# A pre-LN transformer block on one core: x loaded in eight parts, the prologue's statistics and evacuations dealt out anew, a PSUM bank held back

## The chip, the core and the metric

The kernel runs on one core of a Trainium2 chip. The metric is device time in microseconds (us) of one execution, median of several runs. A core has TensorE (PE in the profile; PEld is its weight load), VectorE (DVE), ScalarE (ACT), GpSimd (POOL) and SyncE (SP), which here issues every DMA. The engines run side by side, each takes its own instructions in order, and semaphores tie them together.

## The reference

Sequence 2048, width 640, 32 heads of 20, all in bfloat16:

```python
h  = x + softmax(q k^T / sqrt(20)) v @ wo      # q, k, v = layernorm(x) @ wqkv
h2 = h + (gelu(g) * u) @ w_down                # g, u = layernorm(h) @ w_gate, w_up (width 1728)
```

## The kernel before, in words

**A planner writes the order.** The function declares operations (engine, planned duration, priority, what is read and written, which PSUM banks are taken) and `Sched.schedule` (line 102) plays them out with planned times, taking on each engine the ready operation of lowest priority number; `emit` writes each engine's instructions in that order with the semaphore waits needed. The order is fixed when the kernel is built: on the chip an engine whose next instruction is not ready waits, even if a later one is. Most constants at the file's head are arguments of this planner. A tuple has one value per slot (below).

**Prologue.** x arrives in parts (`load_x`, line 608, in the order `XORD`), then wqk, wv and wo. x is 16 tiles of 128 rows. Tiles are normalised by `GROUPS`: first the statistics of a group, then one reciprocal root for all of it (ScalarE does the root), then each tile is normalised by VectorE (`ln_apply`, "apply" below), transposed by TensorE (line 675) into PSUM and copied out by ScalarE (line 681) or, for the tiles in `XN_DVE`, by VectorE (line 684). Statistics come from VectorE (`bn_stats` twice and `bn_aggr`) at the lowest priority, `P_BG`; for the group `AG` they come from ScalarE (`act_stats`, line 718: a Copy and a Square with an accumulated sum per tile). Warm matmuls (`WN` of them, line 620) fill TensorE before real work. Then the K projection of head block 0 (four chunks of 512 rows, line 758; chunk c needs tiles 4c to 4c+3), copied out by ScalarE (line 795); the largest |K| per row comes from VectorE (line 792), before the copy from PSUM for chunks in `KPS`, after it from SBUF for the others; with `KCUT` chunk 3 is done in two pieces. The maximum over all chunks gives a bound on the scores (`kd`, `sel0`, `q_bound0`), after which the first scores can be computed.

**Slots.** Attention runs in 32 slots: query chunks of 512, 256 (five) and 128 (two) rows by groups of four heads. A slot has 64 score tiles of 128x512, all from line 1081. They are grouped into units of three and two PSUM banks in turn (0 to 2, then 3 and 4); ScalarE computes the exponential of a unit in one instruction. `D_SLOT` blocks of four tiles per slot go to VectorE instead, which builds the exponential from integer arithmetic (line 992 from PSUM, then four terms, each needing its own product with V; `SUMS` says how many pairs VectorE adds first). A VectorE tile is put into a unit's third bank (a "ring", `D_RING` of a slot's twelve) or into a free bank of 5 and 7; those banks also serve all background work: K, Q and V projections, the output projection and the feed-forward of the query chunk before (`post`). `RESV` is a time: where the next unit has a VectorE tile in a bank of its own and is due sooner than that, TensorE takes no other work that would leave banks 5 and 7 without a free one. At 0 the rule is off.

**Tail.** After the last slot, output projection and feed-forward of the last 128 rows.

Of the kernel before, what the change touches and what calls it, by code (L numbers as in the profile page):

```python
# [18 lines left out]
DRAIN = {"pe": 0.165, "act": 0.118, "dve": 0.085, "pool": 0.05, "sp": 0.0}  # L19
WARM_WIN, WARM_MIN = 3.4, 0.5  # L20
PAD_WIN, PAD_MIN = 3.4, 0.42
QK_LEAD = (0.68, 0.72,) + (0.65,) * 4 + (0.72,) * 7 + (0.6,) * 4 + (0.72,) * 6 + (0.68, 0.68, 0.55, 0.55, 0.68, 0.65, 0.65, 0.68, 0.68,)
ACT_GAP = .012
PE_AGE = (2.5,) + (3.0,) * 5 + (5.0,) * 8 + (3.0,) * 3 + (5.0, 5.0, 2.0, 2.0,) + (5.0,) * 4 + (1.5, 1.5, 3.5, 3.0,) + (1.5,) * 3
SD_AGE = (0.6, 0.6, 0.3,) + (0.6,) * 6 + (0.8,) + (0.6,) * 5 + (1.0, 0.3, 0.6, 0.8, 0.6, 1.0, 0.5, 1.0, 1.0, 0.5,) + (0.6,) * 3 + (0.8,) * 4
SD_ROW = (0,) * 5 + (0.6,) * 4 + (1.5, 0.6, 0.6, 1.5,) + (0.6,) * 16 + (1.0, 0.6, 0,)
STOP = None


# [336 lines left out]
NTERM = len(TERMS)  # L366
PV_QUADS = 2
PR, PR2 = 13, 6
D_SLOT = (1,) + (3,) * 26 + (2, 3, 3, 0, 0,)
SUMS = (0,) + (1,) * 4 + (2, 2, 0, 0, 1, 0,) + (1,) * 3 + (0, 1, 1, 2, 3, 1, 0, 1, 1, 0, 2, 2, 1, 0, 1, 0, 3, 0,)  # L370
HOP = 3.2
D_LAT = 0.3
RECIP_MAGIC = float(0x7EF311C3)
COL = 256
WN, WB, WW, WC = 76, (5, 4), 256, 32
KCUT = (384,)
KPS = (2, 3)
P_KM = 1.52
P_VA = 9
RESV = 0.0  # L380
QK_LAT = 0.165
VN = 4
D_RING = (9,) * 4 + (6, 6,) + (9,) * 6 + (6,) * 16 + (12,) + (6,) * 3
D_FIRST = 0
D_SPAN = (16,) + (18,) * 13 + (17,) + (18,) * 4 + (19,) * 4 + (18,) * 7 + (17, 17,)
# [40 lines left out]
LATE = (0, 1, 2, 3, 4)  # L426

# [1 line left out]
def bass_sequential_preLN__mha_block__glu_gated_geglu__prompt_kernel(  # L429
# [10 lines left out]
    x_hbm = A_x[0]  # L440
    out_hbm = out[0]
    with ExitStack() as es:
# [123 lines left out]
        def cst(fn, key, n=128):  # L566
# [149 lines left out]


        def act_stats(t0, n):
            for t in sorted(range(t0, t0 + n), key=lambda t: (XORD.index(t // 4), t)):
                for f, k in ((ACT.Copy, 0), (ACT.Square, 1)):  # L720
                    op("act", I("activation", junk, x_sb[:, t, :], f, accum_out=asum[:, k, t - t0:t - t0 + 1]), 0.86, 1.4,
                       reads=[f"x{t // 4}"], writes=["junk", ("as", t)])
            m = mv[:, t0:t0 + n, 0]
            rk = [("as", t) for t in range(t0, t0 + n)]
            d = lambda fn, r, w: op("dve", fn, 0.17, P_RS, reads=r, writes=w)
            d(I("tensor_scalar", m, asum[:, 0, 0:n], 1.0 / D, None, ALU.mult), rk, ["am"])
            d(I("tensor_tensor", asum[:, 0, 0:n], m, m, ALU.mult), ["am"], rk)
# [194 lines left out]
        for c, (q0, nq) in enumerate(CHUNKS):  # L922
            n = 512 // nq
# [22 lines left out]
        while rem:  # L946
# [3 lines left out]
            k = in_slot.setdefault(s_, [0, 0])  # L950
# [4 lines left out]
            n = len(bs)  # L955
# [567 lines left out]
```

## Time and profile before

| | us |
|---|---|
| median of 3 runs (lowest, highest) | 866.83 (866.38, 867.52) |
| the profiled execution's own time | 867.75 |
| its span, first to last instruction | 866.0 |
| ScalarE busy | 838.4 (97%) |
| TensorE busy | 838.5 (97%) |
| VectorE busy | 750.4 (87%) |

Two engines are busy for 97% of the span. A busy TensorE is not one at its peak (its matmuls overlap and some are fill). Three stretches are to be kept apart: the prologue, up to the first exponential; the slots; the tail.

### The profile page before, as it was taken

The page shows a single profiled execution, that of the slowest core. Times are in us where ns is not written, and L with a number is a line of the kernel's source. Part 1 is how long each engine was busy: PE and PEld are TensorE (multiplying, and loading weights), DVE is VectorE, ACT ScalarE, POOL GpSimd, SP SyncE. Part 2 cuts the span into 40 slices and gives each one's busy share as a digit, 9 for nine tenths or more (in the row PEclk, how much of TensorE's full clock was granted, in tenths as well). Part 3 has the DMA queues.
Part 4 walks back from the last instruction along what each step waited for, and adds up shares of the span by engine and source line. Part 5 has one row for each costly group of instructions (what it writes and reads, how often), then busy time and mean ns, then how long its engine had stood idle before and what let it go on. Part 6 is the DMA issues. An engine that isn't in the chain of part 4 may idle for free.

```text
span 866.0 us, 35545 instructions
## 1 busy us (share of the span) xinstructions
PE 838.5 (97%) x16215; PEld 420.4 (49%) x16215; DVE 750.4 (87%) x1372; ACT 838.4 (97%) x806; POOL 89.6 (10%) x268
## 2 busy tenths in 40 slices
PE   7999999999999899999999999999999999999998
PEld 5532332322343344445455555555554556666667
DVE  8769999999999799797899989999999897988344
ACT  7999999999999999999999999999999999999992
POOL 5001111110001110101002000011102110010000
PEclk9999999999999999999999999999999999999999
DMA  7212021223202642001110102010101101030000
GB/s 274 81 47 61 29 76 47 59 61 92 58 16 60 160 147 80 16 18 36 53 42 16 36 8 61 5 35 17 49 19 24 58 12 27 20 47 11 2 18 17
DMA packets 50173, 43.19 MB, mean 50 GB/s; under 512 B 21316, under 2 KB 44640, under 8 KB 50024
## 3 DMA queue, kind: packets, MB, share of 16 engines
q1 hardware_dynamic: 50024, 40.93, 16.8%
q8 instruction: 127, 2.08, 1.0%
q14 instruction: 22, 0.18, 0.1%
HBM read 27.95 MB, written 10.26 MB: 44 GB/s over the span
## 4 chain that ended last, share of the span: by engine, by line
ACT 51%; PE 39%; DVE 8%; issue 1%
ACT pts L450 35%; ACT rege L450 15%; PE ps L1081 11%; PE ps L450 10%; PE ps L753 9%; PE ps L758 3%; DVE qt_all L450 2%; DVE rege L450 2%; PE ps L907 1%; PE ps L1336 1%; DVE rege L992 1%; DVE qt_all L992 1%; PE ps L1405 1%; ACT qt_all L450 1%; PE ps L675 1%
## 5 line engine op out<-in xcount | busy, mean ns | idle before, releaser
L450 ACT ACTIVATE pts<-ps 128x1024 bf16<-128x1024 f32 (+1 forms) x496 | 558.5, 1240 | 2.8 <-PE ps L1081 2.2
L1081 PE MATMUL ps<-qt_all,kt_all 32*128 32x256 bf16 (+2 forms) x4096 | 304.0, 273 | 11.5 <-ACT pts L450 5.6
L450 ACT ACTIVATE rege<-ps 128x1024 bf16<-128x1024 f32 (+1 forms) x222 | 248.3, 1199 | 0.7 <-PE ps L1081 0.3
L1081 PEld LDWEIGHTS ps<-qt_all,kt_all 32*128 32x128 bf16 x4096 | 103.2, 92 | 202.8 <-ACT pts L450 90.6
L992 DVE TENSOR_SCALAR rege<-ps 128x512 int16<-128x512 f32 x220 | 148.5, 684 | 20.0 <-PE ps L1081 18.6
L450 PE MATMUL ps<-rege,v_all 128*21 128x256 bf16 (+2 forms) x2197 | 139.3, 286 | 0.5 <-DVE rege L450 0.5
L450 PE MATMUL ps<-pts,v_all 128*21 128x256 bf16 (+2 forms) x2403 | 124.8, 273 | 1.0 <-DVE osb L450 0.8
L753 PE MATMUL ps<-rege,regw 128*32 128x256 bf16 (+1 forms) x2600 | 120.5, 296 | 1.6 <-DVE rege L992 0.5
L992 DVE TENSOR_SCALAR qt_all<-ps 128x512 int16<-128x512 f32 x128 | 86.7, 683 | 11.0 <-PE ps L1081 10.2
L450 DVE TENSOR_SCALAR rege<-rege 128x2048 int16<-128x2048 int16 x141 | 94.5, 687 | 1.5 <-PE ps L450 0.8
L753 PEld LDWEIGHTS ps<-rege,regw 128*32 128x32 bf16 x2600 | 60.4, 96 | 34.6 <-issue 20.1
L450 PEld LDWEIGHTS ps<-rege,v_all 128*21 128x21 bf16 x2197 | 54.4, 91 | 41.6 <-issue 26.1
L450 PEld LDWEIGHTS ps<-pts,v_all 128*21 128x21 bf16 x2403 | 56.6, 91 | 26.0 <-issue 19.2
L450 DVE TENSOR_SCALAR qt_all<-qt_all 128x2048 int16<-128x2048 int16 (+4 forms) x113 | 65.4, 589 | 3.0 <-ACT qt_all L450 1.0
L753 PE MATMUL ps<-regw,rege 128*32 128x320 bf16 x1296 | 67.4, 301 | 0.3 <-DVE rege L992 0.3
L758 PE MATMUL ps<-regw 128*128 128x512 bf16 (+2 forms) x215 | 59.6, 368 | 0.4
L450 PE MATMUL ps<-qt_all,v_all 128*21 128x256 bf16 (+1 forms) x1264 | 56.5, 264 | 0.8 <-DVE qt_all L450 0.8
L450 DVE TENSOR_SCALAR qt_all<-rege 128x2048 int16<-128x2048 int16 x80 | 53.8, 684 | 1.6 <-PE ps L450 1.2
L450 POOL TENSOR_SCALAR rn<-rc 128x16 int32<-128x16 int32 x22 | 7.0, 317 | 461.7 <-DMA rc<-sums 461.6
L1390 DVE TENSOR_TENSOR rege<-rege,ps 128x512 bf16<-128x512 bf16 (+2 forms) x53 | 35.0, 661 | 13.0 <-PE ps L753 6.6
L1336 PE MATMUL ps<-rege,regw 128*128 128x128 bf16 (+1 forms) x420 | 40.9, 238 | 0.0
L753 PEld LDWEIGHTS ps<-regw,rege 128*32 128x32 bf16 x1296 | 30.0, 96 | 18.3 <-issue 10.8
(139 smaller groups left out, 805.7 us busy)
## 6 DMA issues: line engine op xcount, KB each, us to landing
bsum<-rsums SPq DMA_DIRECT2D x88, 64.0 KB, 2.1
rege<-in_A_x_dram SPq DMA_DIRECT2D x5, 640.0 KB, 5.8
q_rows<-regw SPq DMA_DIRECT2D x20, 128.0 KB, 1.8
out_dram<-rege SPq DMA_DIRECT2D x15, 160.0 KB, 1.8
regw<-in_B_w_gate_dram SPq DMA_DIRECT2D x5, 432.0 KB, 3.3
regw<-in_B_w_up_dram SPq DMA_DIRECT2D x5, 432.0 KB, 3.5
kt_all<-k_rows SPq DMA_DIRECT2D x12, 160.0 KB
qt_all<-q_rows SPq DMA_DIRECT2D x12, 160.0 KB
```

The costliest lines, as they stand in the source:

```text
L450: return lambda eng: getattr(eng, method)(*args, **kwargs)
L675: op("pe", lambda eng, a=a: eng.transpose(bank16(bk, D)[:, 128 * a:128 * a + 128], src[:, a * 128:(a + 1) * 128], ident[:]), 0.055, prio, ...
L753: return [lambda eng, j=j: eng.matmul(out()[32 * j:32 * j + 32], l[:, 32 * j:32 * j + 32], r, start=start, stop=stop, tile_position=(0, 32 ...
L758: fn = col4(lambda: bank(bk, n), l, r, k == 0, k == len(steps) - 1) if col else lambda eng, l=l, r=r, k=k: eng.matmul(bank(bk, n), l, r, s ...
L907: w_readers.append(op("pe", lambda eng, i=i, kt=kt, a=a: eng.matmul(bank(bk)[:, i * w:i * w + w], xnT[:, a, kt * 128:(kt + 1) * 128], wv[: ...
L992: d_ops.append(op("dve", lambda eng: eng.tensor_scalar(v[:, 512 * h:512 * h + 512], bank(b), EXP_MUL, -32000.0, ALU.mult, ALU.max), c_dve( ...
L1081: return lambda eng: eng.matmul(out()[:, kk * nq:(kk + 1) * nq], kt_all[32 * j:32 * j + 32, g, kt * 128:(kt + 1) * 128], qt_all[32 * j:32 ...
L1336: lambda eng, a=a, f=f, fi=fi: eng.matmul(bank(bk)[:, fi * nq:(fi + 1) * nq], w[:, a, F0[f]:F0[f] + 128], hnT[:, a, 128 * tb:128 * tb + nq ...
L1390: hdone.append(op("dve", lambda eng, bu=bu, fv=fv, w=w: eng.tensor_tensor(fv, fv, bank(bu, w), ALU.mult), c_dve(w), p, reads=[ku] + hkeys( ...
L1405: f == NF - 1) if cl else lambda eng, f=f, o=o, bk=bk, w0=w0, w1=w1: eng.matmul(
```

## The change

All of it is in constants and in the loading of x: no function is new and the planner's code is the same.

- **x in eight parts** of 256 rows in the order 0, 6, 1, 7, 2, 3, 5, 4 (before: four parts of 512 rows in the order 0, 3, 1, 2); a tile's statistics wait for its own part.
- **Statistics.** ScalarE has tiles 12 to 15 (before 11 to 15), VectorE 0 to 11 in groups of four and eight (before 0 to 10, in groups of four and seven).
- **Transposed tiles** 4, 6, 7, 10, 13 and 14 are copied out by VectorE (before 7, 10, 13 and 15).
- **K projection** of block 0: chunk 3 in one piece, and only its maximum is taken from PSUM. The projection of block 1 may start after chunk 1's copy (before: after chunk 3's), its first chunk copied by ScalarE. 60 warm matmuls (before 76).
- **Slots.** Slot 0 gives two blocks to VectorE (before one); more rings in slots 0 and 6 to 10; slot 14 has the pair sum that slot 9 had. `RESV` is 0.4 us. The first query chunk's normalised h is transposed by TensorE (before by DMA). Per-slot lead times and waiting times of the planner (`QK_LEAD`, `PE_AGE`, `SD_AGE`, `SD_ROW`) and several priorities have other values.

```diff
-QK_LEAD = (0.68, 0.72,) + (0.65,) * 4 + (0.72,) * 7 + (0.6,) * 4 + (0.72,) * 6 + (0.68, 0.68, 0.55, 0.55, 0.68, 0.65, 0.65, 0.68, 0.68,)
+QK_LEAD = (0.68, 0.75,) + (0.65,) * 4 + (0.72,) * 6 + (0.68,) + (0.72,) * 3 + (0.6,) * 9 + (0.8,) * 3 + (0.72,) + (0.8,) * 3
...
-D_SLOT = (1,) + (3,) * 26 + (2, 3, 3, 0, 0,)
+D_SLOT = (2,) + (3,) * 26 + (2, 3, 3, 0, 0,)
...
-WN, WB, WW, WC = 76, (5, 4), 256, 32
-KCUT = (384,)
-KPS = (2, 3)
+WN, WB, WW, WC = 60, (5, 4), 256, 32
+KCUT = ()
+KPS = (3,)
...
-RESV = 0.0
+RESV = 0.4
...
-VN = 4
-D_RING = (9,) * 4 + (6, 6,) + (9,) * 6 + (6,) * 16 + (12,) + (6,) * 3
+VN = 1
+D_RING = (8,) + (9,) * 3 + (6, 6,) + (12,) * 4 + (9, 9,) + (6,) * 16 + (12, 6, 6, 4,)
...
-P_EV = 1.8
+P_EV = 1.5
...
-XN_DVE = (7, 10, 13, 15)
+XN_DVE = (4, 6, 7, 10, 13, 14)
...
-XP_PE = (6,)
+XP_PE = (0, 6)
-P_KP = 1.6
-K1_AFTER = 3
-Q1_HOLD = 1
-V_HOLD = 3
+P_KP = 1.5
+K1_AFTER = 1
+Q1_HOLD = 0
+V_HOLD = 6
...
-K1_ACT = ()
+K1_ACT = (0,)
...
-GROUPS = ((0, 4), (4, 7), (11, 5))
-AG = (11, 5)
-P_RS = 1.45
-XORD = (0, 3, 1, 2)
+GROUPS = ((0, 4), (4, 8), (12, 4))
+AG = (12, 4)
+P_RS = 1.0
+XORD = (0, 6, 1, 7, 2, 3, 5, 4)
...
-P_ADD = 1.8
+P_ADD = 0.6
...
-P_OUT = 2.5
+P_OUT = 1.1
...
-            load(x_sb[:, 4 * i:4 * i + 4, :], x_hbm[512 * i:512 * (i + 1), :].rearrange("(t p) d -> p t d", p=128),
-                 f"x{i}", 5.1 + 1.8 * k)
+            load(x_sb[:, 2 * i:2 * i + 2, :], x_hbm[256 * i:256 * (i + 1), :].rearrange("(t p) d -> p t d", p=128),
+                 f"x{i}", 4.2 + 0.9 * k)
```

More of the change, by code (lines that the diff above doesn't have):

```diff
@@ L21 @@
 PAD_WIN, PAD_MIN = 3.4, 0.42
-QK_LEAD = (0.68, 0.72,) + (0.65,) * 4 + (0.72,) * 7 + (0.6,) * 4 + (0.72,) * 6 + (0.68, 0.68, 0.55, 0.55, 0.68, 0.65, 0.65, 0.68, 0.68,)
+QK_LEAD = (0.68, 0.75,) + (0.65,) * 4 + (0.72,) * 6 + (0.68,) + (0.72,) * 3 + (0.6,) * 9 + (0.8,) * 3 + (0.72,) + (0.8,) * 3
 ACT_GAP = .012
-PE_AGE = (2.5,) + (3.0,) * 5 + (5.0,) * 8 + (3.0,) * 3 + (5.0, 5.0, 2.0, 2.0,) + (5.0,) * 4 + (1.5, 1.5, 3.5, 3.0,) + (1.5,) * 3
-SD_AGE = (0.6, 0.6, 0.3,) + (0.6,) * 6 + (0.8,) + (0.6,) * 5 + (1.0, 0.3, 0.6, 0.8, 0.6, 1.0, 0.5, 1.0, 1.0, 0.5,) + (0.6,) * 3 + (0.8,) * 4
-SD_ROW = (0,) * 5 + (0.6,) * 4 + (1.5, 0.6, 0.6, 1.5,) + (0.6,) * 16 + (1.0, 0.6, 0,)
+PE_AGE = (2.5, 3.0, 5.0, 5.0, 2.5, 2.5,) + (3.0,) * 7 + (3.5,) * 4 + (5.0, 5.0, 3.5, 3.5, 5.0,) + (1.5,) * 3 + (5.0,) + (3.0,) * 4 + (1.5, 1.5,)
+SD_AGE = (0.6, 0.6, 0.3,) + (0.6,) * 6 + (0.8,) + (0.6,) * 6 + (0.3, 0.6, 0.8, 0.6, 1.0, 0.5, 1.0, 1.0, 0.5, 0.6, 0.6, 0.8, 0.8,) + (0.6,) * 3
+SD_ROW = (0,) * 5 + (1.0, 0, 0.6, 0.6, 1.5, 0.6, 0.6, 1.5, 0.6, 0,) + (0.6,) * 5 + (0.3, 0.6, 0, 0, 0.6, 0.6, 0.3, 0.6, 0.6,) + (1.0,) * 3
 STOP = None
@@ L368 @@
 PR, PR2 = 13, 6
-D_SLOT = (1,) + (3,) * 26 + (2, 3, 3, 0, 0,)
-SUMS = (0,) + (1,) * 4 + (2, 2, 0, 0, 1, 0,) + (1,) * 3 + (0, 1, 1, 2, 3, 1, 0, 1, 1, 0, 2, 2, 1, 0, 1, 0, 3, 0,)
+D_SLOT = (2,) + (3,) * 26 + (2, 3, 3, 0, 0,)
+SUMS = (0,) + (1,) * 4 + (2, 2,) + (0,) * 4 + (1,) * 6 + (2, 3, 1, 0, 1, 1, 0, 2, 2, 1, 0, 1, 0, 1, 0,)
 HOP = 3.2
@@ L374 @@
 COL = 256
-WN, WB, WW, WC = 76, (5, 4), 256, 32
-KCUT = (384,)
-KPS = (2, 3)
+WN, WB, WW, WC = 60, (5, 4), 256, 32
+KCUT = ()
+KPS = (3,)
 P_KM = 1.52
 P_VA = 9
-RESV = 0.0
+RESV = 0.4
 QK_LAT = 0.165
-VN = 4
-D_RING = (9,) * 4 + (6, 6,) + (9,) * 6 + (6,) * 16 + (12,) + (6,) * 3
+VN = 1
+D_RING = (8,) + (9,) * 3 + (6, 6,) + (12,) * 4 + (9, 9,) + (6,) * 16 + (12, 6, 6, 4,)
 D_FIRST = 0
-D_SPAN = (16,) + (18,) * 13 + (17,) + (18,) * 4 + (19,) * 4 + (18,) * 7 + (17, 17,)
+D_SPAN = (16,) + (18,) * 5 + (17, 17,) + (18,) * 6 + (17,) + (18,) * 4 + (19,) * 4 + (18,) * 7 + (17, 17,)
 D0 = 8
@@ L396 @@
 P_V0 = 2.5
-P_ON = 2.1
+P_ON = 2.4
 V_ACT = (0,)
-XN_DVE = (7, 10, 13, 15)
+XN_DVE = (4, 6, 7, 10, 13, 14)
 VP = (0, 2, 5, 8)
-V1 = ((0, 0, 0, 0, 0, 0, 0, 0, 1, 1, 1, 1, 1, 1, 1, 1), (2, 2, 2, 2, 3, 3, 3, 3, 3, 3, 3, 3, 4, 4, 4, 4))
+V1 = ((1, 1, 1, 1, 1, 1, 1, 1, 1, 1, 1, 1, 1, 1, 1, 1), (3, 3, 3, 3, 3, 3, 3, 3, 4, 4, 4, 4, 4, 4, 4, 4))
 X_LAT = 3.0
@@ L718, in act_stats @@
         def act_stats(t0, n):
-            for t in sorted(range(t0, t0 + n), key=lambda t: (XORD.index(t // 4), t)):
+            for t in sorted(range(t0, t0 + n), key=lambda t: (XORD.index(t // 2), t)):
                 for f, k in ((ACT.Copy, 0), (ACT.Square, 1)):
                     op("act", I("activation", junk, x_sb[:, t, :], f, accum_out=asum[:, k, t - t0:t - t0 + 1]), 0.86, 1.4,
-                       reads=[f"x{t // 4}"], writes=["junk", ("as", t)])
+                       reads=[f"x{t // 2}"], writes=["junk", ("as", t)])
             m = mv[:, t0:t0 + n, 0]
@@ L735, in bass_sequential_preLN__mha_block__glu_gated_geglu__prompt_kernel @@
                 for t in range(t0, t0 + n):
-                    ln_stats(x_sb[:, t, :], t, [f"x{t // 4}"], P_BG)
+                    ln_stats(x_sb[:, t, :], t, [f"x{t // 2}"], P_BG)
             ln_rsqrt(t0, n, P_RS, sqrt=True)
             for t in range(t0, t0 + n):
-                e_ops.append(ln_apply("dve", x_sb[:, t, :], xn_p[:, t % 4, :], ("xnp", t % 4), t, [f"x{t // 4}"], P_PRO))
+                e_ops.append(ln_apply("dve", x_sb[:, t, :], xn_p[:, t % 4, :], ("xnp", t % 4), t, [f"x{t // 2}"], P_PRO))
                 if t in XD:
```

## The prediction, made before the changed kernel was run

> **What bounds the kernel now.** I read the page's busy time first, then that of the stretch between first and last exponential (32.8 to 843 us, thirty windows, their sum quoted), then ScalarE's timeline.
>
> ```profile
> PE 838.5 (97%) x16215; PEld 420.4 (49%) x16215; DVE 750.4 (87%) x1372; ACT 838.4 (97%) x806; POOL 89.6 (10%) x268
> ...
> sum 810.20, PE 791.37 PEld 383.06 DVE 712.17 ACT 806.74 POOL 77.86; mean PE 26.38 PEld 12.77 DVE 23.74 ACT 26.89 POOL 2.60
> ...
> 32.84 5.97 ACT L450 ACTIVATE pts<-ps 128x1536 bf16<-128x1536 f32 x5 [0.23 <-PE ps L1081]
> ...
> 842.35 1.28 ACT L450 ACT_TABLE_LOAD   x1
> ```
>
> In the slots ScalarE is idle for 810.20 - 806.74 = 3.46 us of 810. So the time is three terms: the prologue up to the first exponential (32.84 us), ScalarE's work in the slots with little idle time, and what follows the last exponential (the table load at 842.35 is the tail's first instruction on ScalarE; 866.0 - 842.35 = 23.65 us). TensorE is as busy, but with fill among its work. The change touches the first two terms. For the first I look at VectorE, then at who it waits for.
>
> ```profile
> 4.22 0.48 DVE L450 MEMSET ps<- 128x512 f32 x1
> 6.54 0.48 DVE L450 MEMSET v_all<- 128x512 bf16 x1 [1.84 <-issue]
> 6.65 1.22 DVE L450 BATCH_NORM_STATS2 stats<-rege 128x6 f32<-128x320 bf16 x3
> ...
> 7.89 0.84 DVE L450 BATCH_NORM_STATS2 stats<-rege 128x6 f32<-128x320 bf16 x2
> ...
> 8.75 0.83 DVE L450 BATCH_NORM_STATS2 stats<-rege 128x6 f32<-128x320 bf16 x2
> ...
> 18.86 0.21 DVE L450 BATCH_NORM_AGGREGATE mv<-stats 128x2 f32<-128x12 f32 x1
> ...
> 19.77 0.20 DVE L450 RECIPROCAL rs<-sd 128x7 f32<-128x7 bf16 x1 [0.20 <-ACT sd L450]
> 20.00 0.80 DVE L450 TENSOR_SCALAR rege<-rege,mu,rs 128x640 bf16<-128x640 bf16 x2
> ...
> 21.98 0.45 DVE L450 TENSOR_SCALAR rege<-rege,mu,rs 128x640 bf16<-128x640 bf16 x1 [0.24 <-PE ps L675]
> ...
> 23.24 0.49 DVE L684 COPY regw<-ps 128x640 bf16<-128x640 bf16 x1 [0.23 <-PE ps L675]
> 23.65 0.44 DVE L450 TENSOR_SCALAR rege<-rege,mu,rs 128x640 bf16<-128x640 bf16 x1
> ...
> 25.20 0.49 DVE L684 COPY regw<-ps 128x640 bf16<-128x640 bf16 x1
> 25.61 1.15 DVE L450 TENSOR_SCALAR rege<-rege,mu,rs 128x640 bf16<-128x640 bf16 x3
> 26.83 0.49 DVE L684 COPY regw<-ps 128x640 bf16<-128x640 bf16 x1
> 27.23 0.68 DVE L792 TENSOR_REDUCE km<-regw 128x1 f32<-128x512 bf16 x1
> 27.83 0.48 DVE L684 COPY regw<-ps 128x640 bf16<-128x640 bf16 x1
> ```
>
> From its first statistics at 6.65 to the end of its last apply at 25.61 + 1.15 = 26.76, VectorE waits three times, 0.20 + 0.24 + 0.23 = 0.67 us in 20.11. It is the prologue's bound: the statistics of its eleven tiles end at 18.86 + 0.21 = 19.07, and only then can the second group's root, applies and transposes come. Behind the last apply 32.84 - 26.76 = 6.08 us pass (transposes, last copy, last K chunk, maxima, bound, first scores). ScalarE is not the bound there:
>
> ```profile
> 7.17 0.74 ACT L450 ACTIVATE rege<-rege 128x640 bf16<-128x640 bf16 x1 [1.29 <-DMA rege<-in_A_x_dram]
> ...
> 11.21 0.20 ACT L450 ACTIVATE sd<-sd 128x4 bf16<-128x4 bf16 x1 [1.49 <-DVE sd L450]
> ...
> 20.26 0.19 ACT L450 ACTIVATION_READ_ACCUMULATOR rege<-rege 128x1 f32 x1
> ```
>
> It waits 1.49 us for VectorE's variance at 11.21, and ends its own statistics at 20.26 + 0.19 = 20.45.
>
> **Part by part: the load.** SyncE issues the four loads one after another, and their time from issue to landing is in one row of the view of x's tensor.
>
> ```profile
> 0.78 3.03 SPq L450 DMA_DIRECT2D rege<-in_A_x_dram  x4
> ...
> DMA to landing us min/median/max: 4.7/6.4/8.1
> ```
>
> The first, issued at 0.78, lands at 0.78 + 4.7 = 5.5. VectorE starts on it only at 6.65: before that it sits 1.84 us at a memset that, by the row, waits for nothing the profile names ("issue"). So x was there 1.1 us before it was used. A part of half the size lands earlier still, but nothing says that the memset will come earlier. I cost the earlier load at nothing. Its bounds are 0 and the whole wait, -1.84 us. The four further issues delay the weights' issue by some 3.03 us (four more at 3.03 / 4 each), behind a queue of x; I cost that at nothing too, since VectorE's statistics, not the weights, are late, as shown. ScalarE gains: its first tiles come with the second load of half the size, so its 1.29 us wait at 7.17 shrinks. But it waits for VectorE's variance right after (1.49 us), so this buys nothing by itself.
>
> **VectorE's share.** Unit prices from pitches, since neighbours overlap: one tile of statistics 8.75 - 7.89 = 0.86; one apply 0.80 / 2 = 0.40; one copy of a transposed tile 23.65 - 23.24 = 0.41; one maximum 27.83 - 27.23 = 0.60. What stands ahead of the last apply changes so:
>
> - one tile more of statistics (12, not 11): +0.86;
> - copies: before, two of four (tiles 7 and 10; those of 13 and 15 come at 26.83 and 27.83, behind it). In the change ScalarE's tiles 12 to 15 are done early, as their x comes second and fourth, and the last group is 4 to 11. Ahead are then 13, 14, 4, 6 and 7: five, so 3 x 0.41 = +1.23;
> - maxima: before, all behind the last apply (the first is at 27.23). Now chunks 0 and 3 are complete early and their maxima have a better priority than statistics: 2 x 0.60 = +1.20. If the planner puts them later this is 0.
>
> Sum +3.29 us. Behind the last apply two maxima are left instead of all, but the chain through transposes, ScalarE's copy, projection, copy and maximum of the last chunk is the same in kind; I take -0.3, with -0.6 (one maximum) and 0 as its ends. ScalarE is relieved of a tile's statistics and two copies and gains nothing, because it waits for VectorE already. So the **first exponential comes 3.0 us later**, at 35.8; the ends of the unknowns are +3.3 and 3.0 - 1.84 - 1.20 - 0.67 = -0.7 (start as early as the memset could, maxima behind, no waits). I take the value near the upper end, since each term of it is a counted instruction and each offset only a possibility.
>
> **Warm matmuls.** These rows show what TensorE did around its first transposes, and the granted clock there (the column after busy times).
>
> ```profile
> 12.96 0.45 PE L675 MATMUL ps<-ident,rege 128*128 128x128 bf16 x5 [2.84 <-DVE rege L450]
> ...
> 15.60 3.71 PE L620 MATMUL ps<-zer,ident 128*128 128x256 bf16 x26
> 19.14 0.58 PE L907 MATMUL ps<-regw 128*128 128x160 bf16 x6
> 19.56 2.10 PE L758 MATMUL ps<-regw 128*128 128x512 bf16 x9
> ...
> 14.00:16.00 2.00, 2.00 (x17) 1.76 (x16) 2.00 (x8) 2.00 (x6) 0.00 (x1) 0.50 1.06 394
> ```
>
> Twenty-six fill matmuls stand in front of the first K projection, which starts at 19.56 (nine of 512 columns in 2.10 less an overlap: 0.22 each). Sixteen fewer are worth at most 16 x 3.71 / 26 = 2.3 us there, but chunk 0 isn't the last chunk, so I count nothing.
>
> After the 2.84 us without work the clock was 0.50. The Trainium skill's "TensorE: Matmul & The Clock Gate" (section What's actually happening) says that the array runs at half clock after an idle window of about 3.4 us and needs as long a busy one to recover. The trace agrees in kind: half clock behind an idle stretch, somewhat shorter than that window. It speaks against the change, which takes fill away while VectorE's statistics last longer; by it the sum would gain the cold price given under the rivals.
>
> **The slots.** `D_SLOT` gives four more tiles to VectorE, 1700 - 4 = 1696 are left to ScalarE. The rings turn 3-bank units into 2-bank ones: counted by the unit loop, 95 before and 114 after (+4 in slot 0, +4, +2, +3, +3, +3 in slots 6 to 10). The page's groups of the exponentials, then those of 60 to 141 us with shapes kept apart:
>
> ```profile
> L450 ACT ACTIVATE pts<-ps 128x1024 bf16<-128x1024 f32 (+1 forms) x496 | 558.5, 1240 | 2.8 <-PE ps L1081 2.2
> ...
> L450 ACT ACTIVATE rege<-ps 128x1024 bf16<-128x1024 f32 (+1 forms) x222 | 248.3, 1199 | 0.7 <-PE ps L1081 0.3
> ```
>
> ```profile
> L450 ACT ACTIVATE pts<-ps 128x1024 bf16<-128x1024 f32 x32 | 33.1, 1084 | 0.0
> L450 ACT ACTIVATE pts<-ps 128x1536 bf16<-128x1536 f32 x21 | 31.7, 1511 | 0.0
> L450 ACT ACTIVATE rege<-ps 128x1024 bf16<-128x1024 f32 x17 | 17.3, 1076 | 0.0
> L450 ACT ACTIVATE rege<-ps 128x1536 bf16<-128x1536 f32 x6 | 9.0, 1492 | 0.0
> ```
>
> 496 + 222 = 718 units for 1700 tiles are 264 of three tiles and 454 of two (792 + 908). After: 248 and 476 (744 + 952 = 1696). Durations overlap in the pipeline, so I take pitches: 49 units of two and 27 of three fill 81 us with no idle time ahead of any, and three tiles take 1.511 - 1.084 = 0.427 longer. So a unit of two is (81 - 27 x 0.427) / 76 = 0.914, one of three 1.341. The change: 22 x 0.914 - 16 x 1.341 = **-1.3 us**. Beside it lies more work for the others.
>
> ```profile
> 40.00:60.00 20.00, 19.85 (x191) 8.63 (x190) 13.25 (x23) 20.00 (x20) 0.00 (x0) 1.00 0.29 84
> ```
>
> VectorE has four more tiles in slot 0; between 40 and 60 us it is busy for 13.25 of 20 (third column), which covers them. TensorE has three more products with V there, of about the 0.22 us that a 512-column K matmul takes (above), and in the first post twenty more transposes at 0.45 / 5 = 0.09, which four DMA transposes on SyncE's queue did before; VectorE copies those out, 4 x 0.41 = 1.6 us. I cost all of it at nothing, as part of TensorE's 19.85 us is fill; without that cover it is 0.7 + 1.8 + 1.6 us. What SyncE sends behind the four DMAs can only come sooner.
>
> **The kept bank and the retuned waits.** The trace has no held TensorE, so bounds. VectorE's scores do come late now:
>
> ```profile
> L992 DVE TENSOR_SCALAR rege<-ps 128x512 int16<-128x512 f32 x220 | 148.5, 684 | 20.0 <-PE ps L1081 18.6
> L992 DVE TENSOR_SCALAR qt_all<-ps 128x512 int16<-128x512 f32 x128 | 86.7, 683 | 11.0 <-PE ps L1081 10.2
> ```
>
> VectorE idles 18.6 + 10.2 = 28.8 us for them, in 220 + 128 = 348 tiles, 0.08 each. A held bank can take some of that; but VectorE has slack in the slots and the end is set by ScalarE. What is to be gained is ScalarE's idle time, -3.46 us at most; what can be lost has as its bound a hold of the full 0.4 us for each of 352 - 114 = 238 VectorE tiles with a bank of their own, 95 us of TensorE, of which most would find other work. Between ends so unequal I take a value near the idle row, a fifth more of it: **+0.7**.
>
> **Sum.** +3.0 - 1.3 + 0.7 = +2.4 us. On the profiled execution's 867.75 (866.0 span and 1.75 around it) that is 870.15; the median of the runs is 0.92 below that execution, so **869.2 us**. A measurement here tells about 0.2%, 1.7 us, from no change.
>
> **Rivals.**
>
> 1. *The prologue gets shorter* (faster). One mechanism: VectorE begins as soon as the first small part has landed. The stall at 6.54 then goes (-1.84), the two early maxima fit into its waits or behind (-1.20 and -0.67), so the first exponential is at 32.84 - 0.7 = 32.1, and with the slots' -1.3 and 0.7 of idle time saved the time is 866.83 - 0.7 - 1.3 - 0.7 = 864.1. It decides when the first statistics start before 5.5. For it: x is there at 5.5 already. Against it: the row says that x wasn't what VectorE waited for. 0.32, in which a slot stretch that loses half of its idle time is included.
> 2. *Cancelling* (within 0.2%). The maxima stay behind the last apply: +3.0 - 1.2 - 1.3 = +0.5, 867.3. For it: they stood there before. 0.18.
> 3. *The hold costs* (slower still). TensorE lets its background wait, the work piles up, and scores come late for ScalarE: if one hold in eight is not refilled, 30 x 0.4 = 12 us of TensorE, of which a third reaches ScalarE, +4 on top: 873.2. For it: TensorE is 97% busy. Against it: part of that is fill. 0.12.
> 4. *A cold TensorE at the prologue's end*. Five K matmuls at 0.22 each would take twice that, +1.2, transposes and scores some 0.6 more, +1.8 on the forecast: 871.0. For it: the 0.50 row. Against it: the planner puts fill in. 0.05.
>
> **Chances.** Forecast 0.33, rivals 0.32, 0.18, 0.12, 0.05. Faster by over 0.2%: 0.32; within: 0.18; slower: 0.33 + 0.12 + 0.05 = 0.50. Cases of both signs hold most of it, so the range reaches from a little under the first rival to past the third, 862.5 to 875; the forecast's own is 867.5 to 871.5 (its first exponential between 34 and 36.1).
>
> **What would show it.** First statistics on VectorE at 6.65 again (step one) or earlier. End of the last apply near 30, with two maxima ahead of it. First exponential near 35.8. ScalarE's groups with 476 and 248 members. ScalarE's idle time in the slots near 4.2. I am wrong if the first exponential is under 33.5, or if ScalarE's idle time is far from that.

## The result, and the profile after

| | before, us | after, us |
|---|---|---|
| median of 16 runs each, side by side | 866.87 (866.00 to 867.85) | 868.43 (868.05 to 869.11) |
| ratio, 95% interval | | 1.0018 (1.0010 to 1.0025) |
| the profiled execution's own time, its span | 867.75, 866.0 | 868.76, 867.0 |
| first exponential | 32.84 | 34.31 |
| from there to the tail's table load | 809.51 | 808.96 |
| from there to the end of the span | 23.65 | 23.73 |

The change costs 1.56 us on this chip, just inside the 0.2% that the prediction set as its bound; to an outcome within that bound it gave 0.18, to a slower kernel 0.50. The forecast was 869.2, just beyond the slowest run (869.11). Its stretches came out unevenly: the prologue is 1.47 us longer, not 3.0; the slots are 0.55 shorter, near the forecast sum (-1.3 + 0.7 = -0.6), though not by those two terms. The stretches add up to 1.0 us, as the two profiled executions differ, and not to 1.56: the profiled execution of the kernel before lies 0.88 above its median (more under TensorE's clock, below).

First the two stretches from the first exponential to the table load, for the kernel before and then for the one after (sum of the window, then each engine's busy time in it), with the first exponential and the page's groups of the exponentials after.

```profile
sum 809.51, PE 790.68 PEld 382.51 DVE 711.53 ACT 806.09 POOL 77.86; mean PE 790.68 PEld 382.51 DVE 711.53 ACT 806.09 POOL 77.86
```

```profile
sum 808.96, PE 786.74 PEld 384.76 DVE 713.92 ACT 806.30 POOL 76.88; mean PE 786.74 PEld 384.76 DVE 713.92 ACT 806.30 POOL 76.88
```

```profile
34.31 5.97 ACT L450 ACTIVATE pts<-ps 128x1536 bf16<-128x1536 f32 x5
...
L450 ACT ACTIVATE pts<-ps 128x1024 bf16<-128x1024 f32 (+1 forms) x505 | 560.3, 1214 | 1.8 <-PE ps L1081 0.6
...
L450 ACT ACTIVATE rege<-ps 128x1024 bf16<-128x1024 f32 (+1 forms) x219 | 245.4, 1195 | 0.8 <-PE ps L1081 0.5
```

505 + 219 = 724 units for 1696 tiles are 248 of three and 476 of two, as counted in advance. ScalarE's busy time in the stretch rose by 0.21, and its idle time fell from 3.42 to 2.66. The groups' own busy times (560.3 + 245.4 = 805.7 us, before 558.5 + 248.3 = 806.8) are not ScalarE's time: ScalarE has other work in the stretch too, and where a unit overlaps a neighbour of the other group, both groups count the overlap. What a unit costs is the time from its start to the next instruction's start, idle time included. By the starts in the two traces that is 1.337 us for three tiles before and 1.336 after, and 0.941 for two tiles in both. So 22 more units of two and 16 fewer of three are worth 22 x 0.941 - 16 x 1.337 = -0.7 us, and everything else in the slots, the +0.1 that is left.

Then the prologue on VectorE and ScalarE after the change (start, duration, engine, line, operation, and in brackets the idle time before it with its releaser).

```profile
6.54 0.48 DVE L450 MEMSET v_all<- 128x512 bf16 x1 [1.84 <-issue]
6.65 1.21 DVE L450 BATCH_NORM_STATS2 stats<-rege 128x6 f32<-128x320 bf16 x3
...
20.08 0.67 DVE L792 TENSOR_REDUCE km<-regw 128x1 f32<-128x512 bf16 x1
...
20.75 0.18 DVE L450 BATCH_NORM_AGGREGATE mv<-stats 128x2 f32<-128x12 f32 x1
21.77 0.20 DVE L450 RECIPROCAL rs<-sd 128x8 f32<-128x8 bf16 x1 [0.20 <-ACT sd L450]
22.01 1.16 DVE L450 TENSOR_SCALAR rege<-rege,mu,rs 128x640 bf16<-128x640 bf16 x3
23.10 0.49 DVE L684 COPY regw<-ps 128x640 bf16<-128x640 bf16 x1
...
23.86 0.48 DVE L684 COPY regw<-ps 128x640 bf16<-128x640 bf16 x1
...
24.97 0.48 DVE L684 COPY regw<-ps 128x640 bf16<-128x640 bf16 x1
...
26.79 0.48 DVE L684 COPY regw<-ps 128x640 bf16<-128x640 bf16 x1
27.19 0.80 DVE L450 TENSOR_SCALAR rege<-rege,mu,rs 128x640 bf16<-128x640 bf16 x2
27.90 0.88 DVE L684 COPY regw<-ps 128x640 bf16<-128x640 bf16 x2
...
30.46 0.68 DVE L792 TENSOR_REDUCE km<-regw 128x1 f32<-128x512 bf16 x1
31.05 0.68 DVE L792 TENSOR_REDUCE km<-ps 128x1 f32<-128x512 f32 x1
...
31.85 0.15 DVE L450 TENSOR_REDUCE kd<-km 128x1 f32<-128x4 f32 x1
```

```profile
5.78 0.72 ACT L450 ACTIVATE rege<-rege 128x640 bf16<-128x640 bf16 x1
...
11.35 0.20 ACT L450 ACTIVATE sd<-sd 128x4 bf16<-128x4 bf16 x1 [2.17 <-DVE sd L450]
```

and, from the view of x's tensor after the change, the time from the issue of its loads to their landing:

```profile
DMA to landing us min/median/max: 3.1/5.8/6.9
```

The memset of V's ones stands where it did, and the first statistics start at 6.65 as before. The first of x's eight loads, issued at 0.78, lands 3.1 us later (4.7 before), at 3.9, so x now lies there for 2.8 us unused. ScalarE starts on its own tiles 1.39 us earlier (5.78 against 7.17), does one pass more before the first root (four against three) and spends the rest in a longer wait for VectorE's variance (2.17 against 1.49). Ahead of the last apply stand four copies and one maximum, and it ends at 27.19 + 0.80 = 27.99 (26.76 before). From its last copy (28.78) to the merged maximum `kd` it is 3.07 us; before it was 2.20 (28.31 to 30.51).

### The profile page after: what moved, and what is told of

Same layout as the page of the kernel before. It is cut to its first block, busy times and chain, and to the rows that moved or that the text cites. A ratio compares the mean times of both kernels' runs of the same rounds, so it can differ in the third digit from the quotient of the medians.

```text
span 867.0 us, 35468 instructions
## 1 busy us (share of the span) xinstructions
PE 835.5 (96%) x16142; PEld 421.7 (49%) x16177; DVE 754.9 (87%) x1385; ACT 836.8 (97%) x806; POOL 88.6 (10%) x268
## 4 chain that ended last, share of the span: by engine, by line
ACT 45%; PE 42%; DVE 11%; issue 1%
ACT pts L450 29%; ACT rege L450 14%; PE ps L1081 13%; PE ps L450 10%; PE ps L753 9%; PE ps L758 4%; DVE rege L450 3%; DVE rege L992 3%; PE ps L907 2%; DVE qt_all L450 2%; PE ps L1336 1%; ACT qt_all L450 1%; PE ps L1405 1%; DVE qt_all L992 1%; DVE stats L450 1%
## 5 line engine op out<-in xcount | busy, mean ns | idle before, releaser
L450 ACT ACTIVATE pts<-ps 128x1024 bf16<-128x1024 f32 (+1 forms) x505 | 560.3, 1214 | 1.8 <-PE ps L1081 0.6
L1081 PE MATMUL ps<-qt_all,kt_all 32*128 32x256 bf16 (+2 forms) x4096 | 311.6, 273 | 11.8 <-ACT pts L450 6.1
L450 ACT ACTIVATE rege<-ps 128x1024 bf16<-128x1024 f32 (+1 forms) x219 | 245.4, 1195 | 0.8 <-PE ps L1081 0.5
L1081 PEld LDWEIGHTS ps<-qt_all,kt_all 32*128 32x128 bf16 x4096 | 105.2, 92 | 199.3 <-ACT pts L450 78.6
L992 DVE TENSOR_SCALAR rege<-ps 128x512 int16<-128x512 f32 x224 | 151.4, 685 | 20.0 <-PE ps L1081 18.5
L450 PE MATMUL ps<-pts,v_all 128*21 128x256 bf16 (+2 forms) x2409 | 122.8, 273 | 0.7 <-DVE osb L450 0.5
L450 DVE TENSOR_SCALAR rege<-rege 128x2048 int16<-128x2048 int16 x145 | 97.3, 686 | 1.6 <-PE ps L450 1.1
L758 PE MATMUL ps<-regw 128*128 128x512 bf16 x174 | 51.4, 383 | 2.1 <-issue 1.3
```

Source lines behind the costliest of these rows:

```text
L450: return lambda eng: getattr(eng, method)(*args, **kwargs)
L758: fn = col4(lambda: bank(bk, n), l, r, k == 0, k == len(steps) - 1) if col else lambda eng, l=l, r=r, k=k: eng.matmul(bank(bk, n), l, r, s ...
L992: d_ops.append(op("dve", lambda eng: eng.tensor_scalar(v[:, 512 * h:512 * h + 512], bank(b), EXP_MUL, -32000.0, ALU.mult, ALU.max), c_dve( ...
L1081: return lambda eng: eng.matmul(out()[:, kk * nq:(kk + 1) * nq], kt_all[32 * j:32 * j + 32, g, kt * 128:(kt + 1) * 128], qt_all[32 * j:32 ...
```

## The experiments

The theory after the first look: the prologue is VectorE's, longer by its larger share and with two whole K chunks behind the last copy; the ones hold its start; the slots gain from the other mix of units what their waits leave. Rivals: the kept bank did the slots' part; the eight loads did something by themselves; TensorE's fill did. The first two have runs of their own below; no run changes the number of warm matmuls alone.

**The halves by themselves.** E1 has the changed kernel's constants of the prologue, and all constants that only the slots use are those of the kernel before. E2 is the other half.

```diff
 # E1, against the changed kernel
-D_SLOT = (2,) + (3,) * 26 + (2, 3, 3, 0, 0,)
+D_SLOT = (1,) + (3,) * 26 + (2, 3, 3, 0, 0,)
-RESV = 0.4
+RESV = 0.0
...
```

> The changed kernel's prologue with the slots' constants of before. Theory (the loss is the prologue's, the slots give a little back): first exponential at 34.3 us as in the changed kernel, time 1.5 us above before or a little more (868.3 to 869). Rival (the slots' constants cost the time): first exponential at 34.3 too, but the time within 0.5 us of before.

> The prologue of before with the changed slots' constants. Theory: first exponential at 32.8 us, ScalarE 476 units of two tiles and 248 of three, time 0.5 us below before (866.0 to 866.8). Rival (the slots' constants cost the time): 1 to 1.5 us above before.

E1 took 877.59 us (ratio 1.0115, 1.0102 to 1.0129), E2 893.40 (1.0295, 1.0274 to 1.0316). E1's first exponential is at 34.32, as in the changed kernel. E2's is at 31.94, 0.9 earlier than the 32.8 expected, though VectorE's order up to it is that of the kernel before; the reason is TensorE's clock, below. The times are far from the parts' sum of 1.47 and -0.55. E2's last apply and its first exponential:

```profile
24.72 1.15 DVE L450 TENSOR_SCALAR rege<-rege,mu,rs 128x640 bf16<-128x640 bf16 x3
...
31.94 5.97 ACT L450 ACTIVATE pts<-ps 128x1536 bf16<-128x1536 f32 x5 [0.23 <-PE ps L1081]
```

ScalarE's waits, with total, times and longest in us, first of E2 and then of the kernel before:

```profile
ACT pts L450 <- PE ps L1081: 16.1, 10, 9.9
ACT qt_all L1359 <- PE ps L1336: 11.9, 4, 7.5
```

```profile
ACT qt_all L1359 <- PE ps L1336: 6.3, 4, 1.9
...
ACT pts L450 <- PE ps L1081: 2.2, 6, 0.7
```

In E2 one unit of scores near 130 us is 9.9 us late: SyncE sends the bound of the next head groups 13.7 us later than in the kernel before. Its rows, E2 first:

```profile
137.35 0.59 SPq L450 DMA_DIRECT2D qt_all<-bounds  x1
```

```profile
123.62 0.58 SPq L450 DMA_DIRECT2D qt_all<-bounds  x1
```

And in both halves the tail grows, to 30.3 us in E1 and 32.3 in E2 from 23.7; in E2's rows above, ScalarE waits 11.9 us in it for the feed-forward's matmuls (line 1336), against 6.3. A new theory: the many planner constants are fitted to one exact order, and anything that perturbs the order costs more than what is being measured.

**A perturbation that computes nothing new.** E5 is the kernel before with the planner's assumed landing of x 0.1 us later. The work is the same; only the planner's choices of order differ.

```diff
-                 f"x{i}", 5.1 + 1.8 * k)
+                 f"x{i}", 5.2 + 1.8 * k)
```

> The kernel before with one planned duration moved: x's landing times in the planner 0.1 us later. Nothing that is computed or loaded changes, only the order that the planner writes. Theory (each set of per-slot constants fits one exact order, and the three mixed kernels lost that fit, not time of their own mechanism): first exponential within 0.5 us of 32.8, but the time 5 to 20 us above before, with long single waits of ScalarE in the slots and a longer tail. Rival (the mixed kernels lost time by the constants themselves): time within 2 us of before.

883.87 us, ratio 1.0180 (1.0166 to 1.0194). The prologue is like before (first exponential 33.02); the rest is waits and a tail of 33.9 us. This bears the theory of the fitted order out: in the six runs with another order (E1, E2, E3, E5 and, below, E11 and E12) the time is 10 to 26 us above the kernel before, 6 to 17 times the change itself. So from here on a run is read either by its total, where the order on TensorE, ScalarE and VectorE is kept but for the edited instruction, or by its prologue alone.

**What is projected ahead of K.** E3 puts the holds of Q and V back (their casts of 0.60 and 0.56 us stand among the last maxima after the change).

```diff
-Q1_HOLD = 0
-V_HOLD = 6
+Q1_HOLD = 1
+V_HOLD = 3
```

> The changed kernel with Q1_HOLD and V_HOLD of before, so that the copy of the second Q projection (0.60 us) and of a V projection (0.56 us) on VectorE, and the absolute value that follows (0.24 us), wait for the bound. Theory (VectorE's work is what the prologue is made of): first exponential 1.2 to 1.4 us earlier, near 33.0, time about 1 us below the changed kernel (867.4). Rival (the last K chunk's projection on TensorE sets the end): first exponential at most 0.4 us earlier.

886.16 us (1.0213, 1.0199 to 1.0227). The first exponential, which the expectation was about, is at 35.62, 1.31 later, not earlier: in this order a copy of a projection (line 800, at 33.72) and a table load stand right ahead of it on ScalarE. The scores themselves start at 33.94, where the changed kernel has them at 33.87. So the casts had filled a wait: without them VectorE waits for K's last chunks instead:

```profile
30.21 0.69 DVE L792 TENSOR_REDUCE km<-regw 128x1 f32<-128x512 bf16 x1 [0.94 <-ACT regw L795]
...
35.62 5.97 ACT L450 ACTIVATE pts<-ps 128x1536 bf16<-128x1536 f32 x5
```

**The ones of V.** E4 gives their memset in the changed kernel to GpSimd; E7 gives it to ScalarE in the kernel before; E9 does the same in the changed kernel.

```diff
 # E4
+        cst(I("memset", v_all[:, :, :, DH:DH + 1], 1.0), "vones", 512)
 # E7 and E9
+        op("act", I("activation", v_all[:, :, :, DH:DH + 1].rearrange("p t h o -> p (t h o)"), nw[:, 0, 0:1].to_broadcast([128, NT * H]), ACT.Copy, scale=2.0), 0.001, 2.0, reads=["half"], writes=["vones"])
 # all three
-        op("dve", I("memset", v_all[:, :, :, DH:DH + 1], 1.0), 0.6, P_QK, writes=["vones"])
```

> The changed kernel with the ones of V's extra column written by GpSimd instead of VectorE. Theory (VectorE bound, and its 1.84 us without work belong to that memset): first statistics near 4.8 us, first exponential 1.3 to 1.8 us earlier, near 32.7, time 867. Rival 1 (the stall belongs to something else in front of the statistics): first statistics at 6.5 still, no change in time. Rival 2 (the statistics start early but another engine holds the prologue): first statistics near 4.8 and first exponential within 0.4 us of 34.3.

> The kernel before with the ones of V's extra column written by ScalarE, in its wait for x, instead of VectorE; the order of all else is the same. Theory (the 1.84 us belong to that memset, and x's first part lands at 5.5): first statistics near 5.6 us, first exponential about 1 us earlier (31.8) or somewhat more, time about 1 us below before (865.9). Rival (ScalarE's root or the K chain holds the prologue): first exponential within 0.3 us of 32.84.

> The changed kernel, with the ones of V written by ScalarE instead of VectorE (the twin of the run that did so in the kernel before); the order on every engine is otherwise the same. Theory: what holds the changed kernel's VectorE until 6.65 us is the write of the ones, so its first statistics start near 4.6, and as VectorE had only 0.85 us of waits up to the score bound, most of the 2 us come through: first exponential 34.31 to 32.3-32.8 (GpSimd as the writer brought 1.03 with VectorE blocked for 1.9 us further on). Time against the kernel before 0.999 to 1.000, that is 866 to 867. Rival: ScalarE's own statistics, which start 2 us later behind the ones, become the bound of the prologue, as its share there is nearly as large as VectorE's: first exponential 33.5 or later, time 1.001.

| | first statistics | first exponential | us | ratio to before (95%) |
|---|---|---|---|---|
| E4, changed, GpSimd | 4.61 | 33.28 | 868.04 | 1.0005 (0.9996 to 1.0014) |
| E9, changed, ScalarE | 4.61 | 33.93 | 868.14 | 1.0006 (0.9997 to 1.0015) |
| E7, before, ScalarE | 5.19 | 30.65 | 866.21 | 0.9981 (0.9973 to 0.9990) |

The stall at 6.54 was the ones: with them gone VectorE starts 1.5 to 2.0 us earlier, and in E7 it now waits for x, 0.48 us. E7's ratio is the lowest of all runs here, below both kernels. In the changed kernel less of it arrives. In E9 VectorE waits for x (0.49 us) and then for a root: ScalarE needs 1.96 us for the ones (6.50 to 8.46) and has no idle time left ahead of that root. In E4 VectorE stands while GpSimd writes: three small instructions, of which the neighbours take 0.2 to 0.5 us, end together with the write. The two statistics just before them (14.35 to 15.18) overlap the write and are not slowed, so the first that is held is the `tensor_scalar`; the other two stand behind it in VectorE's order. The rows are VectorE's in E9, then in E4, then GpSimd's in E4.

```profile
11.42 0.18 DVE L450 RECIPROCAL rs<-sd 128x4 f32<-128x4 bf16 x1 [0.84 <-ACT sd L450]
```

```profile
15.10 1.93 DVE L450 TENSOR_SCALAR mv<-asum 128x4 f32<-128x4 f32 x1
15.16 1.87 DVE L450 BATCH_NORM_AGGREGATE mv<-stats 128x2 f32<-128x12 f32 x1
15.28 1.75 DVE L450 BATCH_NORM_STATS2 stats<-rege 128x6 f32<-128x320 bf16 x1
```

```profile
14.64 2.37 POOL L450 MEMSET v_all<- 128x512 bf16 x1
```

For E9 the rival holds (33.93, where it said 33.5 or later): with the ones added, ScalarE is as late as VectorE, so relief of one at the cost of the other helps little. On the chip that timed E9, the changed kernel's own order (E10, below) took 868.63, so the ones are worth 0.49 us there.

**The eight loads alone.** E6 is the kernel before with eight loads in its own order (the two halves of each part in turn); the order on every engine but SyncE is kept. E8 adds E7's edit.

```diff
-            load(x_sb[:, 4 * i:4 * i + 4, :], x_hbm[512 * i:512 * (i + 1), :].rearrange("(t p) d -> p t d", p=128),
-                 f"x{i}", 5.1 + 1.8 * k)
+            for j in range(2): load(x_sb[:, 4 * i + 2 * j:4 * i + 2 * j + 2, :], x_hbm[512 * i + 256 * j:512 * i + 256 * j + 256, :].rearrange(
+                "(t p) d -> p t d", p=128), f"x{2 * i + j}", 5.1 + 1.8 * k - 0.08 * (k + j))
```

> The kernel before with only the load of x in eight parts, in the same sequence of rows, with the planned times kept, so that every engine but SyncE has the same instructions in the same order. Theory (VectorE doesn't wait for x): first statistics at 6.65 us, first exponential within 0.2 us of 32.84, time within 0.1% of before. Rival (smaller transfers pay by themselves, either way): first exponential moved by 0.5 us or more.

> Both of the two edits before: x in eight parts and the ones by ScalarE, in the order of before. Theory (only without the memset do the smaller parts buy something): first statistics near 4.7 us, first exponential 0.5 to 0.9 us earlier than with the ones alone, so near 31.0, time 1.8 us below before (865). Rival: no earlier than with the ones alone.

E6 took 868.22 us (1.0006, 0.9997 to 1.0015), E8 866.59 (0.9990, 0.9981 to 0.9998). Where the ones hold VectorE, an earlier x is worth nothing. Where they don't (E8 against E7), it starts 0.58 us earlier, but the first exponential is 0.47 later (31.12 against 30.65), since the weights of the first projection come behind eight loads; so the rival holds. TensorE in E8:

```profile
17.34 0.59 PE L907 MATMUL ps<-regw 128*128 128x160 bf16 x6 [0.69 <-DMA regw<-in_A_wqkv_dram]
```

**What E6 shows by the way: TensorE's clock in the prologue.** E6's first exponential is at 32.01, although its order is that of the kernel before, at 32.84. The difference begins at TensorE. E6:

```profile
2.92 7.99 PE L620 MATMUL ps<-zer,ident 128*128 128x256 bf16 x47 [2.92 <-POOL ident L450]
12.95 0.45 PE L675 MATMUL ps<-ident,rege 128*128 128x128 bf16 x5 [2.04 <-DVE rege L450]
...
14.91 3.05 PE L620 MATMUL ps<-zer,ident 128*128 128x256 bf16 x26
17.80 0.58 PE L907 MATMUL ps<-regw 128*128 128x160 bf16 x6
18.43 1.89 PE L758 MATMUL ps<-regw 128*128 128x512 bf16 x8
```

and the changed kernel:

```profile
2.92 7.03 PE L620 MATMUL ps<-zer,ident 128*128 128x256 bf16 x43 [2.92 <-POOL ident L450]
12.94 0.45 PE L675 MATMUL ps<-ident,rege 128*128 128x128 bf16 x5 [2.99 <-DVE rege L450]
...
15.48 2.82 PE L620 MATMUL ps<-zer,ident 128*128 128x256 bf16 x15
18.35 2.10 PE L758 MATMUL ps<-regw 128*128 128x512 bf16 x9
```

The first warm matmuls, the same in every execution of a kernel, take 6.2 to 8.0 us in the profiles here, so the idle stretch behind them varies. In the six profiles (E1, E2, E4, E6, E7, E8) where it was 0.78 to 2.34 us the granted clock stayed 1.00; in the eight (both kernels, E3, E5, E9, E10, E11, E12) where it was 2.77 to 3.83 it fell to 0.5 for 3.4 us. The rows of 14 to 16 us (granted clock third from the end), E6 and then the changed kernel:

```profile
14.00:16.00 2.00, 1.92 (x23) 1.64 (x22) 2.00 (x8) 2.00 (x6) 0.00 (x0) 1.00 1.05 394
```

```profile
14.00:16.00 2.00, 1.81 (x15) 1.59 (x15) 2.00 (x8) 2.00 (x6) 0.00 (x0) 0.53 1.06 395
```

A half clock for 3.4 of 866 us makes a mean granted clock of 0.998, none of it 1.000, and the profiled executions of both kernels, E4, E6, E7, E8, E9 and E10 have just these means, so for these kernels each timed run tells which it was. On one chip 21 runs of the kernel before at 0.998 have a mean of 868.13 us and 6 at 1.000 one of 867.23; on another it is 867.75 (12 runs) and 866.87 (3). The cold stretch costs the kernel before **0.9 us**, as the prologues of E2 and E6 say too, and 54 of its 63 executions beside the experiments paid it. The changed kernel is cold in 15 of its 16 runs, but its 15 fill matmuls in place of 26 let the first K projection start at 18.35 even so (19.56 before, 18.43 in E6). Its one warm run took 868.24, inside the spread of the others (mean 868.49), and E1, which is warm, has its first exponential at the same place (34.32), though in another order from about 25 us on. So the cold stretch seems to cost the changed kernel little. That the shorter fill is what takes the 0.9 back is argued, not shown: VectorE's longer share, which lets the next transposes start only at 22.62 (21.50 before), hides a late K projection as well. E12, below, speaks for the fill: cold, with 15 fill matmuls and the old shares, its last apply ends at 25.51 (26.76 before), but its order differs in other things too.

The Trainium skill's "TensorE: Matmul & The Clock Gate" (section What's actually happening) says that the window of about 3.4 us is free-running, so that the switch comes at another place from run to run. The clock records in the traces agree: the half clock lasts 3.4 us in each of the eight prologues, and full clock is first granted at 5.55 to 8.65 us, at another time in each profile that has such records (E6's has none). A whole idle window was not needed here, though: 2.77 us of idle time were enough in E11, and of the 3.4 us ahead of its switch at 14.60 only 1.7 (11.2 to 12.94) belong to that idle stretch.

By the same reading E7's gain over the kernel before can be split: at 0.998 it is 866.87 (5 runs) against 868.13, at 1.000 it is 865.91 (6) against 867.23. The ones are worth 1.3 us at like clock; the rest of the 1.73 is that more of its runs stay at the full clock. E6 is 0.5 to 0.6 slower than the kernel before at like clock (868.65 and 867.81): the eight loads cost that, not in the prologue but in the slots (810.74 us from 32.01 to the table load, against 809.51, one profile each). Why there was not found.

**The kept bank.** With `RESV = 0` the planner gives the changed kernel the same order on every engine, so that E10 is the changed kernel once more.

```diff
-RESV = 0.4
+RESV = 0.0
```

> The changed kernel with RESV = 0. The theory of this run: the kept bank changes no instruction's place, so this is the changed kernel again: ratio 1.0018 within 0.0008 of it, first exponential 34.3, 2.6 to 2.7 us of idle time on ScalarE in the slots, 476 and 248 units. The rival, that keeping the bank is worth the 0.8 us of idle time that the changed kernel has less (3.46 to 2.65): idle time near 3.5, ratio 1.0027.

868.63 us, ratio 1.0007 (0.9998 to 1.0016). From 34.38 to the table load at 843.44:

```profile
sum 809.06, PE 793.01 PEld 384.19 DVE 714.00 ACT 806.20 POOL 77.53; mean PE 793.01 PEld 384.19 DVE 714.00 ACT 806.20 POOL 77.53
```

2.86 us of idle time on ScalarE: 0.56 of the 0.76 less than before is there without the bank, and the rest is between two executions of one order. The rule is in the code, and at 0.4 us it moves no instruction. The run also says how sure the verdict is: the same program stood at +1.56 us on one chip and +0.82 on another; only 1.0010 to 1.0016 lies in both intervals. The clock may be part of that: on the first chip the times of the kernel before fall into 9 from 866.00 to 866.87 and 7 from 867.36 to 867.85, on the second all 21 were cold. For the first chip's 16 no clock is on record, so this is argued, not shown. Where both are known to be cold, the change costs 0.8 us (E10's 11 runs) or 1.0 (the two profiled executions).

**K's last chunk, and the shares.** E11 cuts it in two again; E12 has the shares of before.

```diff
 # E11
-KCUT = ()
-KPS = (3,)
+KCUT = (384,)
+KPS = (2, 3)
 # E12
-XN_DVE = (4, 6, 7, 10, 13, 14)
+XN_DVE = (7, 10, 13, 15)
-GROUPS = ((0, 4), (4, 8), (12, 4))
-AG = (12, 4)
+GROUPS = ((0, 4), (4, 7), (11, 5))
+AG = (11, 5)
```

> The changed kernel with the last K chunk in two parts again (KCUT = (384,), KPS = (2, 3)). Theory: of the 1.47 us by which the first exponential is late, 1.0 lies behind the last transposed tile's copy, because two whole K chunks are projected there; with 384 columns of the last chunk projected ahead, the bound is through 0.7 to 1.0 us sooner: first exponential 33.3 to 33.6. Rival: those 384 columns need tiles that are copied last too, so nothing moves: 34.2 to 34.4. By the theory of the fitted order the slots' order, which changes from the score bound on, is no longer the tuned one, so the time is 875 to 890 whatever the prologue does.

> The changed kernel with the statistics and copies shared as before (11 tiles on VectorE, 5 on ScalarE; copies of tiles 7, 10, 13, 15 on VectorE). Theory: the changed share costs what VectorE gets, 0.86 of statistics and two to three copies ahead of the last apply: first exponential 1.0 to 1.7 us earlier, 32.6 to 33.3. Rival: in the changed kernel VectorE's and ScalarE's shares end together (waits of 0.85 us on VectorE), so the old share makes ScalarE, with a fifth tile at two passes of about 0.8, the late one: 34 to 35. By the theory of the fitted order the time is 875 to 890 again.

881.80 us (1.0159, 1.0144 to 1.0175) and 890.73 (1.0268, 1.0252 to 1.0284), in or next to the band that the fitted order gave. The prologues are read at `kd`, E11 first:

```profile
31.44 0.15 DVE L450 TENSOR_REDUCE kd<-km 128x1 f32<-128x5 f32 x1
...
34.56 5.97 ACT L450 ACTIVATE pts<-ps 128x1536 bf16<-128x1536 f32 x5 [0.73 <-PE ps L1081]
```

```profile
24.36 1.15 DVE L450 TENSOR_SCALAR rege<-rege,mu,rs 128x640 bf16<-128x640 bf16 x3
...
29.29 0.16 DVE L450 TENSOR_REDUCE kd<-km 128x1 f32<-128x4 f32 x1
...
37.97 0.75 DVE L895 SCALAR_TENSOR_TENSOR qt_all<-ps,off,qt_all 128x512 bf16<-128x512 f32 x1 [4.25 <-DMA qt_all<-regw]
```

E11: `kd` 0.41 earlier, then a V cast of 0.65 stands ahead of the bound and the first exponential is not earlier (34.56). So the cut is worth 0.4 at most, not the 0.7 to 1.0 expected, and here nothing. E12: the last apply ends at 25.51, 2.48 earlier, and `kd` comes 2.56 earlier, more than the 1.0 to 1.7 expected. Then the bound waits 4.25 us for a transfer that SyncE issues behind twelve of K's, and the first exponential is at 39.43; neither expectation had that. SyncE in E12:

```profile
27.04 8.95 SPq L450 DMA_DIRECT2D kt_all<-regw  x12
36.02 0.71 SPq L450 DMA_DIRECT2D qt_all<-regw  x1
```
The share is the large term of the prologue; what E12 would take with an order made for it stays open.

## Why the prediction was right or wrong

- **The load at nothing** (step one): right. The first statistics are at 6.65 again, and the reason given, that VectorE waited for something other than x, is shown: E4 and E9 move the ones and it starts at 4.61. That the statement held is also why the first rival fell. Its condition (statistics before 5.5) is met in E4 and E9, and they gain 1.03 and 0.38 us of the prologue, not the 2.2 that separate the rival's 32.1 from what was measured.
- **VectorE's share, +3.29:** mis-sized. Against E2, whose prologue is that of the kernel before at full clock and whose last apply ends at 24.72 + 1.15 = 25.87, the changed kernel's 27.99 is 2.12 later. One tile of statistics, two more copies and one maximum at the prediction's own prices are 0.86 + 0.82 + 0.60 = 2.28. The step that failed is the order: it had ScalarE's tiles 12 to 15 normalised early and tiles 4 to 11 last. By the order that the planner writes, the last copies, at 27.90, are those of tiles 13 and 14, so a copy that was counted ahead stands behind, and chunk 3 with its maximum is last, not early. Five copies and two maxima were four and one: 0.41 + 0.60 too much.
- **Behind the last apply, -0.3:** wrong in sign, +0.24 (34.31 - 27.99 = 6.32 against 6.08). One maximum fewer is left there, but two whole K chunks come after the last copy.
- **Warm matmuls at nothing:** wrong, about -0.9. The prediction saw the 0.50 row and priced a cold array as a risk of the change. The kernel before already paid it: its VectorE, called the prologue's bound, waits for transposes that stand behind a late chunk 0 on TensorE, and its last apply ends 0.89 later than E2's. "Chunk 0 isn't the last chunk" overlooked them. In the changed kernel the price does not show; that the shorter fill removes it is argued, as said above. In sum 3.0 - 1.01 - 0.16 + 0.54 - 0.90 = 1.47, the measured prologue: two miscounted instructions, 2.28 - 2.12, the term behind the last apply, and the cold stretch (32.84 against E2's 31.94).
- **The slots, -1.3 + 0.7:** the counts of units were right, the two terms were not. The price of a unit of two tiles came from 60 to 141 us, 0.914; over the whole stretch it is 0.941, so the counts are worth -0.7, and everything else +0.1. The sum of -0.6 was met by luck, by two errors of 0.6 that cancel. ScalarE's idle time, which the prediction wanted near 4.2 and named as a sign of being wrong, went to 2.66: by that sign this part was wrong.
- **The kept bank:** its price was taken as part of the +0.7; E10 shows that it has none.
- **Not foreseen:** that the constants are fitted to one exact order. The prediction took the retuned waits into one +0.7 and ended its range at 875; E1, E2, E3, E5, E11 and E12 lie 10 to 26 us above the kernel before, all of them past that end. That the change stays near the kernel before because its set of constants is fitted too is the reading that these runs suggest.
- **The total:** 869.2 against 868.43 is closer than the stretches are. The prediction took over the 0.92 us between the profiled execution and the median of the kernel before; in the changed kernel they are 0.33 apart (868.76 and 868.43), which makes up for 0.6 of the prologue's error of 1.5. That is luck too.

## What to carry to other kernels

When an engine sits at an instruction that waits for nothing, move that instruction before making its inputs earlier: in the kernel before, the eight loads gave nothing and the ones moved to ScalarE gave 0.19%. A schedule whose constants were fitted to one order can't be taken apart edit by edit; test an edit there with the order kept, or read only the stretch ahead of the point where the orders part. Before crediting a change with a gain, look at whether the kernel before pays a price of its own, such as the cold array here, that the edit may happen to remove.

## What the runs showed of the hardware

- Writing 128x512 bf16 ones with a stride of 21 elements held each of three engines for 2.0 to 2.4 us: VectorE 1.95 (4.70 to 6.65, though the memset's own row reads 0.48), ScalarE 1.96 (6.50 to 8.46), GpSimd 2.37.
- While GpSimd wrote them (14.64 to 17.01), VectorE's small instructions begun at 15.10 to 15.28 all ended at about 17.03: 1.93 us for one of 128x4 elements. Statistics that ran from 14.35 to 15.18 were not slowed.
- An idle stretch of 2.77 us (E11) was followed by the half clock on TensorE, one of 2.34 (E1) was not; the half clock lasted 3.4 us each time, and the same kind of warm matmuls ran for 6.2 to 8.0 us from one profile to the next.
